# Windowed attention in unsplit fp32 on half arrays, its weights turned on VectorE and through DRAM

## The chip, the cores and the metric

One core of a Trainium2 chip runs the whole program: TensorE (PE, with its weight loads shown apart as PEld), VectorE (DVE), ScalarE (ACT), GpSimd (POOL) and SyncE (SP, which issues most transfers). The metric is device time in microseconds (us). The kernel before took 868.0 us, the median of three runs between 867.7 and 868.03.

## The reference

Attention over 4 sequences of 576 tokens, 8 heads of 64, with a causal window of 128 tokens and a linear bias, and then a dense mixture of 4 experts over the 2304 tokens of width 512:

```python
scores = scale * np.matmul(q, k.transpose(0, 1, 3, 2))
mask = (rel >= 0) & (rel < window)                      # window = 128
scores = np.where(mask, scores + bias[None], -1000000000.0)
attn = np.exp(scores - np.max(scores, axis=-1, keepdims=True))
attn = attn / (np.sum(attn, axis=-1, keepdims=True) + 1e-09)
x = np.matmul(attn, v)            # then heads side by side: (2304, 512)
for e in range(E):                # 4 experts, F = 1024
    h = np.maximum(x @ w1[e], 0.0)
    out += p[:, e:e + 1] * (h @ w2[e])
```

## The kernel before

**Split products.** TensorE multiplies one-pass "fp32r" operands here. To keep fp32 accuracy an operand is split into a rounded high part (a cast, `cast`, L380 on ACT or L381 on DVE) and the remainder (`minus`, L400 on DVE or POOL), and a product is the sum of several one-pass products of parts.

**Tiles.** The 2304 tokens stand in 18 tiles of 128 queries, and these in seven blocks (`BLOCKS`: three of 256 tokens, four of 384). Four head pairs times seven blocks make 28 segments (`segment`), each of two or three units (`unit`): one tile of queries for two heads. A unit's keys are its own tile and the 128 before it (fewer at a sequence's start). The first block is "plain": its four segments already use unsplit fp32 operands with 64 rows a head (L679) and 64 output columns a head (L921 with `acc,v`). The other 24 segments, with 64 units, are the ones in question.

**A unit before the change.** Scores: four one-pass matmuls (L688), per head the high and the low keys against queries whose high and low parts are stacked on 128 rows. `copy_predicated` (L742) folds the keys of the tile before and the own tile into 128 columns, since every query sees exactly 128 of the 256. DVE adds the bias and takes the least (L751), ACT takes the exponential (L769), and the weights are scaled by the reciprocal of their sum (L799 on DVE or L806 on ACT). TensorE transposes the two 128x128 blocks (L824) into a PSUM bank; a cast and a `minus` take the high and low parts out, and two POOL selects (L862) unfold them into `pt`, one for the tile before and one for the own tile. Values (L921): per head one-pass products of both parts of `pt` with `vs`, the high and low values side by side in 128 columns; the two halves of the output are added afterwards (ACT L948, DVE L951). Blocks 4 to 6 share accumulators in chains (`CHAINS`).

**The experts.** The first products (L1300, L1392) and second products (L1803) run in the same program order, and later passes use seven products in place of eight (L1449, L1699); DVE and POOL make the sums and remainders for them. These matmuls fill TensorE between the attention's.

**What sets the order.** Every operation is recorded in a `Plan` with its duration, its due time and what it reads and writes. `order()` then simulates the engines and emits each engine's instructions in the order that it finds; on the chip every engine runs its list in that order and waits by semaphores. SP issues its transfers in the listed order too. `FILL` = 80 small bf16 matmuls on `ones` (L1870) are put where the plan leaves TensorE free.

Of the kernel before, what the change touches and what calls it, by code (L numbers as in the profile page):

```python
# [27 lines left out]
class Buf:  # L28


    def __init__(self, tag):
        self.tag, self.place, self.uses, self.done, self.free = tag, None, 0, 0, 0.0
# [5 lines left out]
class Op:  # L38
    __slots__ = ("n", "engs", "emit", "due", "deps", "outs", "wait", "ready", "bufs", "cold", "start", "end", "eng", "port", "late", "lag", "after", "made")


class Plan:
# [12 lines left out]
    def op(self, engs, emit, due, reads=(), writes=(), holds=(), cold=None, port=None, late=0.0, lag=0.0, after=()):  # L55
# [5 lines left out]

        o.port, o.late, o.lag = (POOL,) if port is None else port, late, lag
# [27 lines left out]
    def order(self):  # L90
        at = dict.fromkeys((PE, DVE, ACT, POOL, SP), 0.8)
        queue = {e: [] for e in at}
        bus = port = 0.0
        landed = [0.0] * FLIGHT
# [7 lines left out]
        def slots(o):  # L102

            t, taken = -1.0, []
            for b in o.bufs:
                if b.place is not None:
                    continue
# [18 lines left out]
        while len(out) < len(self.ops):  # L126
            best = None
            for e, q in queue.items():
                cands, least = [], None
                for o in q:  # L130
# [3 lines left out]
                    t = max(at[e], o.ready[e], s[0] + 0.2 if s[1] else 0.0)  # L134
# [6 lines left out]
                if least is None:  # L141
                    continue
                t, o, taken = min(
                    (c for c in cands if c[0] <= least + SLACK), key=lambda c: (c[1].due, c[1].n)
# [33 lines left out]
            new = [b for b in o.bufs if b.place is None]  # L178
            for b, (tag, i) in zip(new, taken):
                owner[tag][i] = b  # L180
                b.place = self.places[tag][i]
# [14 lines left out]
AGAIN = 8.82  # L196
# [3 lines left out]
PLAIN = 4.0  # L200
FLIGHT = 9
SLACK = 0.1
PATIENCE = 0.4
HOLDOFF = 12.0
OPENS = 4.0
FAR = 3.0
EXTRA = 0.03
LATE_S = 2.02
LATE_T = .5
LATE_V = 1.34  # L210
# [27 lines left out]

CHAIN = (4, 5, 6)
CHAINS = ((2, (4,)), (3, (4,)), (0, (4, 5, 6)), (1, (4, 5, 6)), (2, (5, 6)), (3, (5, 6)))  # L240
ALONE = (0, 1, 2), (0, 2, 4), (1, 3, 5)
HEAD = (1, 2, 3), (0, 2, 4), (1, 3, 5)
PLACES = {
    1: (ALONE,),
    2: (HEAD, ALONE),
    3: (HEAD, ((0, 1, 2), (0, 2, 4), (1, 3, 1)), ((3, 0, 1), (4, 2, 1), (3, 0, 5))),
}
# [24 lines left out]
def attention_moe(  # L272
# [30 lines left out]
    def places(tag, n, shape, dt, pool_=sb):  # L303
# [10 lines left out]
    places("s", 3, [P, 2, 2 * P], F32)  # L314
    places("t", 6, [P, 6], F32)
    pt = sb.tile([P, 2, 2, 2 * QN], F32R, tag="pt", name="pt")
    plan.places["th"], plan.places["tl"] = (
        [plan.places[t][i][:, :, :QN] for t in ("qs", "kh", "kl")] + [pt[:, 0, i, :].rearrange("p (k n) -> p k n", k=2)]
        for i in range(2)
    )  # L320
    plan.places["s7"] = [pt[:, 1], vs[:].rearrange("p i t a d -> p i (t a d)")[:, :, :768]]
# [187 lines left out]
    turns = [(nb, hp) for hp, nbs in CHAINS for nb in nbs]  # L509
    for nb, (s0, n) in enumerate(BLOCKS):  # L510
        for hp in range(NPAIR):
# [4 lines left out]
            mine = next((c for h, c in CHAINS if h == hp and nb in c), (nb,))  # L516
            g.turn = turns.index((nb, hp)) if nb in CHAIN else -1
            g.open, g.behind, g.over = nb != mine[-1], nb != mine[0], None
            g.cols, g.prev, g.own = PLACES[len(mine)][mine.index(nb)]
            g.kn, g.vn = s0 + n - g.k0, (s0 + n) // P - g.v0 - g.open  # L520
            for i in range(n // P):
# [6 lines left out]
                if nb in CHAIN:  # L528
                    lo_, hi_ = spans[CHAIN[0]][0], spans[CHAIN[-1]][1]
                    at_ = turns.index((nb, hp)) * (n // P) + i  # L530
                    u.due = lo_ + (hi_ - lo_) * at_ / (len(CHAIN) * NPAIR * (n // P)) - MARGIN
                else:
                    u.due = lo_ + (hi_ - lo_) * (hp * (n // P) + i) / (NPAIR * (n // P)) - (MARGIN if nb else 0)
# [3 lines left out]

    for g in gs:
        if g.behind:
            g.over = next(x for x in gs if x.nb == g.nb - 1 and x.hp == g.hp)  # L540
# [16 lines left out]
    def segment(g):  # L557
# [4 lines left out]
        if g.plain:  # L562
            if g.hp % 2 == 0:
                shared = Buf("k"), Buf("v"), Buf("av")
# [6 lines left out]
            g.av = Part(shared[2], lambda t: t.place[half], half)  # L571
        else:
            k, v = g.k, g.v = Buf("k"), Buf("v")
        g.qs, g.kh, g.kl, g.vs = Buf("qs"), Buf("kh"), Buf("kl"), Buf("vs")
# [15 lines left out]
        else:  # L590
            q, g.qo = Buf("q"), 0
            g.q = q
            load(
                lambda: k[r, :, :kn],
                lambda: kd[hs, r, g.k0 : g.k0 + kn].rearrange("h p c -> p h c"),
                8 * r.stop * kn,
                due - 6,
                ["qk"],
                [k],
            )  # L600
            load(
                lambda: q[r, :, :n],
                lambda: qd[hs, r, g.s0 : g.s0 + n].rearrange("h p c -> p h c"),
                8 * r.stop * n,
                due - 6,
                ["qk"],
# [1471 lines left out]
```

## Time and profile before

| what | value |
|---|---|
| median of three runs | 868.0 us |
| profiled execution, span | 866.3 us |
| PE busy | 860.7 us (99%) |
| DVE, ACT, POOL busy | 706.9, 491.1, 494.6 us |
| PE's share of the chain that ended last | 97% |

The span is the profiled execution's own time from its first to its last instruction; the page has no other time for that execution, and the 1.7 us between span and median are what lies around it and between executions. A row of instructions on TensorE gives the start, and a length that holds the time through the array as well; since matmuls follow each other before the one ahead has come out, the time that one costs is the distance to the next start, not its length.

### The profile page before, as it was taken

The page shows a single profiled execution, that of the slowest core. Times are in us where ns is not written, and L with a number is a line of the kernel's source. Part 1 is how long each engine was busy: PE and PEld are TensorE (multiplying, and loading weights), DVE is VectorE, ACT ScalarE, POOL GpSimd, SP SyncE. Part 2 cuts the span into 40 slices and gives each one's busy share as a digit, 9 for nine tenths or more (in the row PEclk, how much of TensorE's full clock was granted, in tenths as well). Part 3 has the DMA queues.
Part 4 walks back from the last instruction along what each step waited for, and adds up shares of the span by engine and source line. Part 5 has one row for each costly group of instructions (what it writes and reads, how often), then busy time and mean ns, then how long its engine had stood idle before and what let it go on. Part 6 is the DMA issues. An engine that isn't in the chain of part 4 may idle for free.

```text
span 866.3 us, 15295 instructions
## 1 busy us (share of the span) xinstructions
PE 860.7 (99%) x5154; PEld 785.7 (91%) x5154; DVE 706.9 (82%) x1610; ACT 491.1 (57%) x1231; POOL 494.6 (57%) x696
## 2 busy tenths in 40 slices
PE   9999999999999999999999999999999999999998
PEld 6999888888888889999989899899899999999998
DVE  7888777778787887878998887876878888788877
ACT  7877666567777686753444434443346554545542
POOL 4665776465667767564552222522755776586663
PEclk9999999999999999999999999999999999999999
DMA  8676654444444555222597566545374446345602
GB/s 271 197 256 195 215 181 142 126 133 134 146 141 149 174 154 173 68 77 88 194 368 270 192 259 219 211 156 206 131 256 149 132 157 219 126 131 183 196 25 73
DMA packets 52526, 148.87 MB, mean 172 GB/s; under 512 B 4960, under 2 KB 22112, under 8 KB 48736
## 3 DMA queue, kind: packets, MB, share of 16 engines
q1 hardware_dynamic: 46592, 118.35, 40.5%
q0 software_dynamic: 5632, 29.36, 10.4%
q8 instruction: 40, 0.66, 0.3%
q14 instruction: 38, 0.31, 0.1%
q10 hardware_dynamic: 224, 0.20, 0.1%
HBM read 112.23 MB, written 35.65 MB: 171 GB/s over the span
## 4 chain that ended last, share of the span: by engine, by line
PE 97%; DVE 1%; DMA 0%; SPq 0%; issue 0%; ACT 0%; DVEq 0%
PE b L1803 31%; PE b L1449 23%; PE b L1392 18%; PE b L1699 11%; PE av L921 4%; PE b L688 3%; PE b L824 2%; PE av L1699 2%; PE av L1449 1%; PE b L1870 1%; PE b L1300 1%; DVE xl L400 0%; DVE acc L1725 0%; PE b L679 0%; DMA k<-in_qk 0%; SPq L373 0%
## 5 line engine op out<-in xcount | busy, mean ns | idle before, releaser
L1803 PE MATMUL b<-w2h,halves 128*128 128x512 f32 x612 | 214.1, 397 | 0.0
L1392 PE MATMUL b<-xh,w 128*128 128x512 f32 (+2 forms) x576 | 160.4, 344 | 0.0
L1803 PEld LDWEIGHTS b<-w2h,halves 128*128 128x128 f32 x612 | 115.1, 188 | 20.8
L1821 DVE SCALAR_TENSOR_TENSOR acc<-b,prob,acc 128x512 f32<-128x512 f32 x136 | 101.3, 746 | 32.6 <-PE b L1803 32.0
L1803 PE MATMUL b<-w2l,halves 128*128 128x512 f32 x306 | 120.0, 392 | 0.0
L1392 PEld LDWEIGHTS b<-xh,w 128*128 128x128 f32 x576 | 102.7, 189 | 10.1
L1392 PE MATMUL b<-xl,w 128*128 128x512 f32 (+2 forms) x288 | 97.7, 339 | 0.0
L400 POOL TENSOR_TENSOR w<-w1r,w 128x256 fp32r<-128x256 f32 x86 | 64.4, 773 | 55.0 <-ACT w L380 16.6
L862 POOL TENSOR_SCALAR_AFFINE_SELECT pt<-s 128x512 fp32r<-128x512 f32 x120 | 77.0, 666 | 31.6 <-DVE s L400 12.8
L400 POOL TENSOR_TENSOR w2l<-w2r,w2h 128x256 fp32r<-128x256 f32 x80 | 59.0, 759 | 59.3 <-ACT w2h L380 32.2
L1462 ACT ACTIVATE s<-b 128x384 f32<-128x384 f32 x87 | 42.6, 490 | 71.5 <-PE b L1449 68.9
L1725 DVE SCALAR_TENSOR_TENSOR acc<-b,prob,acc 128x256 f32<-128x256 f32 x135 | 58.5, 475 | 11.5 <-PE b L1699 9.9
L769 ACT ACTIVATE s<-s,t 128x128 f32<-128x128 f32 x128 | 50.4, 395 | 29.7 <-DVE t L751 28.4
L1803 PEld LDWEIGHTS b<-w2l,halves 128*128 128x128 f32 x306 | 57.7, 188 | 7.7
L1349 ACT ACTIVATE halves<-b 128x256 fp32r<-128x256 f32 (+2 forms) x76 | 36.8, 485 | 47.0 <-PE b L1392 46.4
L1449 PE MATMUL b<-xh,w 128*128 128x384 f32 x200 | 59.3, 337 | 0.0
L1392 PEld LDWEIGHTS b<-xl,w 128*128 128x128 f32 x288 | 54.5, 189 | 4.7
L380 ACT ACTIVATE w2h<-w2r 128x512 fp32r<-128x512 f32 x93 | 55.9, 621 | 3.2 <-PE b L1803 2.5
L1356 DVE SCALAR_TENSOR_TENSOR halves<-b,halves 128x256 fp32r<-128x256 f32 (+2 forms) x76 | 41.9, 553 | 15.8 <-ACT halves L1349 15.1
L380 ACT ACTIVATE w<-w1r 128x512 fp32r<-128x512 f32 x75 | 44.3, 623 | 6.7 <-DVE w1r L1234 4.4
L921 PEld LDWEIGHTS av<-pt,vs 128*128 128x128 f32 x312 | 43.7, 189 | 3.3
L400 DVE TENSOR_TENSOR w2l<-w2r,w2h 128x512 fp32r<-128x512 f32 x62 | 46.2, 758 | 0.3 <-ACT w2h L380 0.2
(249 smaller groups left out, 2460.0 us busy)
## 6 DMA issues: line engine op xcount, KB each, us to landing
w2r<-in_w SPq DMA_DIRECT2D x59, 512.0 KB, 3.5
w1r<-in_w SPq DMA_DIRECT2D x43, 512.0 KB, 4.3
w<-parked POOLq DMA_DIRECT2D x16, 1024.0 KB, 5.3
parked<-w SPq DMA_DIRECT2D x13, 1024.0 KB, 4.7
q<-in_q SPq DMA_DIRECT2D x16, 384.0 KB, 3.6
k<-in_k SPq DMA_DIRECT2D x12, 512.0 KB, 4.5
vs<-parked POOLq DMA_DIRECT2D x8, 768.0 KB, 4.8
pt<-parked POOLq DMA_DIRECT2D x8, 768.0 KB, 4.7
```

Of the source, the lines that this page charges most:

```text
L380: return nc.scalar.activation(o(), i(), AF.Copy)
L400: by[e].tensor_tensor(out=x, in0=y, in1=f(z), op=ALU.subtract) for x, y, z in pieces(e, n, o(), a(), b())
L769: return lambda e: nc.scalar.activation(sv()[:, h, -m:], sv()[:, h, -m:], AF.Exp, bias=t[:, h : h + 1], scale=-1.0, accum_out=t[:, 2 + h : ...
L862: return lambda e: nc.gpsimd.affine_select(out=pt[:, :, :, c0 : c0 + P], in_=hl(), pattern=[[0, 4], [1, P] if own else [-1, P]], base=0, c ...
L921: nc.tensor.matmul(o_, v2, p_, start=not g.started[h], stop=True, skip_group_check=True)
L1392: nc.tensor.matmul(bk[:, :n], a[0][:, kt, fs], b[:, kt, cols], start=kt == 0 and i == 0, stop=kt == KT - 1 and i == 2,)
L1449: nc.tensor.matmul(bank[:, :n], x(k), y(k), start=new and k == 0 and i == 0, stop=k == 1 and i == 2, skip_group_check=True,)
L1462: {ACT: act(n)}, lambda e: nc.scalar.activation(pv(p), bank[:, :n], AF.Copy), at[0] - URGENT, [bank], [p]
L1699: nc.tensor.matmul(bank[bk][part]()[:, cs], a()[:, ns], b()[:, fi, :], start=new and i != 1 and fi == 0 and j == 0, stop=fi == 1 and j == ...
L1725: nc.vector.scalar_tensor_tensor(out=ac[:, ds], in0=bank[bk][part]()[:, cs], scalar=prob[:, nt, e_ : e_ + 1], in1=ac[:, ds], op0=ALU.mult, ...
L1803: nc.tensor.matmul(bk[:, cs], a[:, ns], b[1][:, fi, cs], start=half != 1 and fi == 0 and j == 0, stop=half != 0 and fi == 1 and j == 2, sk ...
L1821: nc.vector.scalar_tensor_tensor(out=o, in0=i_, scalar=p, in1=o, op0=ALU.mult, op1=ALU.add)
```

## The change

Per unit of the 24 segments that are not plain:

- Queries and keys are no longer split. Their loads bring each head's 64 rows once (head 0 on rows 0 to 63, head 1 on rows 64 to 127), and scores are two unsplit fp32 matmuls on 64 rows each, one a head (L649 of the new program), each into its own bank. One planned operation does two neighbouring units.
- The transposes on TensorE are gone. DVE turns the weights in 32x32 blocks (`nc.vector.transpose`), the result goes to a DRAM scratch `tr`, and four transfers read it back with the blocks in their turned places. POOL's two selects then unfold it into `pb` without a split.
- Values are unsplit fp32 matmuls with 64 output columns a head (L903), all of a segment in one planned operation at its last unit, into one PSUM bank; nothing has to be added afterwards. Chains are gone.
- All eight PSUM banks are in the pool `b`.
- The planner knows three modes of TensorE ("full", "row", "col"), counts `SWITCH` for a change of mode, and while in a half-array mode prefers other half-array work (`STICK`). A dozen of its constants have other values. The expert products are the same instructions in the same numbers.

```diff
-    places("b", 6, [P, 512], F32, ps)
-    av = [[ps.tile([P, 512], F32, tag=f"av{h}", name=f"av{h}") for h in range(2)]]
-    plan.places["av"] = av
+    places("b", 8, [P, 512], F32, ps)
+    places("tr", TURNS, [P, 2 * P], F32, dr)
...
+                t, o, taken = min(
                     (c for c in cands if c[0] <= least + SLACK),
+                    key=lambda c: (c[1].due + (0.0 if c[1].mode == "full" else -STICK if sticks else lone), c[1].n),
                 )
...
+                if e == PE and t >= WARM:
+                    o.end += SWITCH if o.mode != mode else 0.0
+                    mode = o.mode
...
+            both = lambda t, c, m: t[hs].rearrange("h p c -> (h p) c")[64:192, c : c + m]
+            load(lambda: k[:, 0, :kn], lambda: both(kd, g.k0, kn), 512 * kn, due - 6, ["qk"], [k])
+            load(lambda: q[:, 0, :n], lambda: both(qd, g.s0, n), 512 * n, due - 6, ["qk"], [q])
...
-        cast(lambda: g.kh[:, :, :kn], lambda: k[:, :, :kn], 2 * kn, due, [k], [g.kh])
-        cast(lambda: g.qs[:, :, :n], lambda: q[:, :, :n], 2 * n, due, [q], [g.qs])
-        minus(
...
-                for m in (g.kh, g.kl):
+            for x in mine:
+                c0 = 0 if g.plain else 2 * P * (x.q0 // P % 2)
+                for h in range(2):
                     r = (lo64, hi64)[h]
+                    qv, kv = (g.q, g.k) if g.plain else (g.q[:, 0], g.k[:, 0])
                     nc.tensor.matmul(
+                        scored[h][:, c0 : c0 + x.pk + P],
+                        qv[r, g.qo + x.q0 : g.qo + x.q0 + P],
+                        kv[r, x.k0 : x.k0 + x.pk + P],
...
+                plan.op(
+                    {DVE: dve(2 * P) + 0.02},
+                    lambda e: nc.vector.transpose(
+                        turned_().rearrange("p (b h c) -> p h b c", b=4, h=2), sv().rearrange("p h (b c) -> p h b c", b=4)
+                    ),
...
+                load(lambda: tr[:], turned_, 131072, d + 0.8, [(wb, b_) for b_ in range(4)], [tr])
+                for b_ in range(4):
+                    load(
+                        lambda b_=b_: wb.place[32 * b_ : 32 * b_ + 32, :].rearrange("r (a n) -> r a n", a=4),
+                        lambda b_=b_: tr[:, 64 * b_ : 64 * b_ + 64].rearrange("(a r) n -> r a n", a=4),
+                        32768,
...
+            if pk:
+                for own in (0, 1):
+                    plan.op({POOL: 0.47}, side(own), d + 0.95 + 0.2 * own, raws_, [(g.pt, 2 * i + own)])
...
+                    d_ = (lo64, hi64)[h]
+                    p_ = g.pt[h][:, c : c + m] if g.plain else turned(c // P, (c + m) // P, h)
+                    nc.tensor.matmul(
+                        g.av[d_, q0 : q0 + m],
+                        g.v[:, vt, d_],
+                        p_,
...
-LATE_V = 1.34
+LATE_V = 1.699
```

TensorE's list before, among the experts' second products (L1803, with `halves` the hidden layer). L688 is one unit's scores, L921 values and L824 another unit's two transposes:

```order
L688 MATMUL b_116<-kh_71,qs_69 128x256
L688 MATMUL b_116<-kl_73,qs_69 128x256
L688 MATMUL b_116<-kh_71,qs_69 128x256
L688 MATMUL b_116<-kl_73,qs_69 128x256
L1803 MATMUL b_117<-w2h_99,halves 128x512
L1803 MATMUL b_117<-w2l_101,halves 128x512
L1803 MATMUL b_117<-w2h_99,halves 128x512 x2
L1803 MATMUL b_117<-w2l_101,halves 128x512
L1803 MATMUL b_117<-w2h_99,halves 128x512
L921 MATMUL av_119<-pt,vs 128x128 x2
L921 MATMUL av_120<-pt,vs 128x128 x2
L824 MATMUL b_115<-ident,s_76 128x128 x2
```

Scores, values and transposes came a unit at a time, with expert matmuls between. After, at a place among first products (L1338, the former L1392):

```order
L1338 MATMUL b_117<-xh_89,w_97 128x512
L903 MATMUL b_116<-pb_85,v_67 64x128 x2
L903 MATMUL b_116<-pb_85,v_67 64x256 x4
L903 MATMUL b_116<-pb_85,v_67 64x128 x2
L649 MATMUL b_121<-k_66,q_64 128x256
L649 MATMUL b_119<-k_66,q_64 128x256
L649 MATMUL b_118<-k_65,q_63 128x128
L649 MATMUL b_120<-k_65,q_63 128x128
L649 MATMUL b_118<-k_65,q_63 128x256
L649 MATMUL b_120<-k_65,q_63 128x256
L1338 MATMUL b_115<-xh_89,w_98 128x512
```

A whole segment's values (L903, eight matmuls) now stand right ahead of the scores of three units (L649, six matmuls), then experts follow; no transposes are left here. Over the whole list the 24 segments' values are 24 runs of column-half matmuls and their scores 25 runs of row-half matmuls, and these 49 runs stand in 27 blocks between full-array matmuls that are not there for a plain segment's values already. Of the 80 fillers on `ones`, 34 stand ahead of the last plain values (60 before), 29 in later places (20 before), and 17 behind the last expert matmul (none before).

SP's list before, early among the attention, with weight loads (`in_w`) and a segment's queries, keys and values:

```order
L373 DMA w1r_92<-in_w 128x1024
L373 DMA v_68<-in_v 128x384
L373 DMA q_63<-in_q 128x2x256
L373 DMA w2r_94<-in_w 128x1024
L373 DMA k_65<-in_k 128x2x384
L373 DMA w1r_93<-in_w 128x1024
L373 DMA w2r_95<-in_w 128x1024
L373 DMA v_67<-in_v 128x384
```

The same stage after; `tr` is the DRAM scratch, `s` the turned weights:

```order
L393 DMA tr_122<-s_77 128x256
L393 DMA w2r_96<-in_w 128x1024
L393 DMA k_65<-in_k 128x384
L393 DMA q_63<-in_q 128x256
L393 DMA tr_123<-s_78 128x256
L393 DMA w1r_93<-in_w 128x1024
L393 DMA s_77<-tr_122 32x4x64 x4
L393 DMA w2r_95<-in_w 128x1024
L393 DMA tr_124<-s_78 128x256
L393 DMA s_78<-tr_123 32x4x64 x2
```

Between the same loads stand a unit's store to the scratch and its four loads back, 320 issues in all, and the loads of queries and keys have half the size. In the stretch shown, a weight load is queued behind every load back, which itself waits for its store to land.

## Rows read from the trace of the kernel before

**Rows 1.** The page: span, busy time by engine, the chain that ended last.

```profile
span 866.3 us, 15295 instructions
...
PE 860.7 (99%) x5154; PEld 785.7 (91%) x5154; DVE 706.9 (82%) x1610; ACT 491.1 (57%) x1231; POOL 494.6 (57%) x696
...
PE 97%; DVE 1%; DMA 0%; SPq 0%; issue 0%; ACT 0%; DVEq 0%
```

**Rows 2.** Windows: stretch, us, busy us (instructions) by engine, clock, DMA share, GB/s.

```profile
0.00:26.00 26.00, 24.39 (x178) 17.90 (x179) 19.46 (x86) 20.07 (x64) 12.41 (x26) 1.00 0.83 267
26.00:391.00 365.00, 365.00 (x2125) 320.85 (x2125) 297.51 (x825) 253.81 (x733) 235.08 (x348) 1.00 0.49 155
```

**Rows 3.** PE groups by form: instructions, count | busy us, mean ns | idle.

```profile
L921 PE MATMUL av<-pt,vs 128*128 128x256 f32 x184 | 29.4, 282 | 0.0
L688 PE MATMUL b<-kh,qs 128*128 128x256 f32 x104 | 28.7, 297 | 0.0
...
L824 PE MATMUL b<-ident,s 128*128 128x128 f32 x128 | 24.6, 273 | 0.0
...
L921 PE MATMUL av<-pt,vs 128*128 128x128 f32 x128 | 17.9, 262 | 0.0
```

**Rows 4.** Timeline, PE: a unit's scores between experts. Start, us, what.

```profile
209.34 0.28 PE L688 MATMUL b<-kh,qs 128*128 128x256 f32 x1
...
209.82 0.39 PE L1803 MATMUL b<-w2h,halves 128*128 128x512 f32 x1
210.05 0.39 PE L1803 MATMUL b<-w2l,halves 128*128 128x512 f32 x1
```

**Rows 5.** Timeline, PE: a unit's two transposes.

```profile
202.44 0.38 PE L824 MATMUL b<-ident,s 128*128 128x128 f32 x2
202.58 0.48 PE L1392 MATMUL b<-xh,w 128*128 128x512 f32 x1
202.89 0.40 PE L1392 MATMUL b<-xl,w 128*128 128x512 f32 x1
```

**Rows 6.** Timeline, PE: four narrow values.

```profile
200.62 0.56 PE L921 MATMUL av<-pt,vs 128*128 128x128 f32 x4
201.02 0.45 PE L1392 MATMUL b<-xh,w 128*128 128x512 f32 x1
201.31 0.39 PE L1392 MATMUL b<-xl,w 128*128 128x512 f32 x1
```

**Rows 7.** Timeline, PE: plain scores of one pair, 128 columns.

```profile
12.68 0.49 PE L679 MATMUL b<-k 64*128 64x128 f32 x4
13.10 0.44 PE L824 MATMUL b<-ident,acc 128*128 128x128 f32 x2
```

**Rows 8.** Timeline, PE: fillers, plain values, plain scores, experts.

```profile
14.14 0.49 PE L1870 MATMUL b<-ones 128*128 128x256 bf16 x3
14.56 0.99 PE L921 MATMUL av<-acc,v 128*64 128x256 f32 x8
15.49 0.70 PE L679 MATMUL b<-k 64*128 64x256 f32 x4
16.12 0.39 PE L1300 MATMUL b<-xh,w 128*128 128x256 f32 x1
16.34 0.28 PE L1300 MATMUL b<-xl,w 128*128 128x256 f32 x1
```

**Rows 9.** Groups by form, DVE: remainders of the transposed weights.

```profile
L400 DVE TENSOR_TENSOR s<-b,s 128x256 fp32r<-128x256 f32 x60 | 25.2, 420 | 1.4 <-ACT s L380 0.5
```

**Rows 10.** DMA issues: count, size, median us to landing.

```profile
aside<-x SPq DMA_DIRECT2D x8, 192.0 KB, 1.9
...
ident<-in_ident SPq DMA_DIRECT2D x1, 64.0 KB, 2.7
dp<-in_dp SPq DMA_DIRECT2D x1, 36.0 KB, 4.0
```

**Rows 11.** Timeline, SP: an issue that waits for nothing.

```profile
6.17 0.43 SPq L373 DMA_DIRECT2D w1r<-in_w  x1
```

More of the change, by code (lines that the diff above doesn't have):

```diff
@@ L38 @@
 class Op:
-    __slots__ = ("n", "engs", "emit", "due", "deps", "outs", "wait", "ready", "bufs", "cold", "start", "end", "eng", "port", "late", "lag", "after", "made")
+    __slots__ = ("n", "engs", "emit", "due", "deps", "outs", "wait", "ready", "bufs", "cold", "start", "end", "eng", "port", "late", "lag", "after", "made", "mode")
 class Plan:
@@ L93, in order @@
         bus = port = 0.0
+        mode = "full"
         landed = [0.0] * FLIGHT
@@ L105, in slots @@
             for b in o.bufs:
-                if b.place is not None:
+                if b.slot is not None:
+                    t = max(t, b.since)
                     continue
@@ L177, in order @@
                 o.end += o.lag
-            new = [b for b in o.bufs if b.place is None]
+            new = [b for b in o.bufs if b.slot is None]
             for b, (tag, i) in zip(new, taken):
+                b.since = owner[tag][i].free if owner[tag][i] else -1.0
                 owner[tag][i] = b
-                b.place = self.places[tag][i]
+                b.slot = self.places[tag][i]
             for b in o.bufs:
@@ L195 @@
 CLOSE = 1.0
-AGAIN = 8.82
+AGAIN = 1.498
 DBW = 2.4e5
@@ L515, in attention_moe @@
             g.v0 = g.k0 // P
[L516 to L520, printed above, removed]
+            g.kn, g.vn = s0 + n - g.k0, (s0 + n) // P - g.v0
             for i in range(n // P):
@@ L697, in unit @@
-        passes_ = PLAIN if g.plain else 4
-        plan.op({PE: passes_ * mm(n)}, scores, d, qk, [*scored, "scores"], [s], passes_ * mmc(n), late=late)
+        qk = [(g.shared[0], g.hp % 2, h) for h in range(2)] if g.plain else [g.q, g.k]
+        if mine:
+            plan.op(
+                {PE: sum(PLAIN * mm(x.pk + P) for x in mine)},
+                scores,
+                d,
+                qk,
+                [*scored, "scores"],
+                [] if not g.plain else [s],
+                sum(PLAIN * mmc(x.pk + P) for x in mine),
+                late=late,
+                mode="row",
+            )
@@ L870, in side @@
                 )
-            plan.op({POOL: 0.79}, side(0), d + 1.1, both, [("pt", g.prev[i])])
-            plan.op({POOL: 0.59}, side(1), d + 1.2, both, [("pt", g.own[i])])
+            if pk:
+                for own in (0, 1):
+                    plan.op({POOL: 0.47}, side(own), d + 0.95 + 0.2 * own, raws_, [(g.pt, 2 * i + own)])
+            else:
+                cast(
+                    lambda: spread(2 * i + 1),
+                    lambda: wb.place,
+                    2 * P,
+                    d + 1.0,
+                    raws_,
+                    [(g.pt, 2 * i + 1)],
+                )
@@ L924, in unit @@
+                    d_ = (lo64, hi64)[h]
[4 more added lines that the diff above has]
+                        p_,
+                        start=not g.started[h],
+                        stop=True,
+                        skip_group_check=True,
+                    )
+                    g.started[h] = True
         if jobs:
+            if g.plain:
+                ps_ = [(b_, k_) for j in jobs for k_ in j[4] for b_ in g.pt]
+            else:
+                ps_ = [(g.pt, x) for x in range(2 * len(g.units)) if x or g.units[0].pk]
```

422 lines of the change are left out of this document (160 added, 262 removed).

## The prediction

> **What bounds the kernel now.** I read the page first. It gives a span of 866.3 us in which TensorE is busy for 860.7, and TensorE holds 97% of the chain that ended last [rows 1]. The windows say the same by stage: in the stretch with attention, 26 to 391 us, TensorE is busy for all of its 365.0 us at the full granted clock (1.00, the 2.4 GHz level), while DVE is at 297.5, ACT at 253.8 and POOL at 235.1 [rows 2]. So nothing but TensorE's own work, and what would make it wait, counts there; work that leaves DVE, ACT and POOL is worth nothing by itself. Only the first 26 us have another limit, since there TensorE partly runs fillers. Then I counted the attention's matmuls by form [rows 3] and took their prices from the timeline, as distances between starts [rows 4 to 8].
>
> **TensorE's work that goes.** Four score matmuls of 256 columns start at 209.34 and the next expert matmul at 209.82, which then takes its usual 0.23 (to 210.05): 0.48 a unit [rows 4]. Of the 64 units 52 have this form (104 matmuls with `kh`, two a unit [rows 3]): 25.0 us. The other 12 have 192 or 128 keys; I price them at 0.43, between four narrow matmuls (0.40) and 0.48: 5.2 us. Two transposes take from 202.44 to 202.58, and the expert matmul behind them needs 0.31 to the next start where 0.23 is usual: 0.14 + 0.08 = 0.22 a unit [rows 4, 5], and 128 of them [rows 3] are 64 pairs: 14.1 us. Values of 256 columns are 184, 46 fours at the 0.48 of the same shape: 22.1 us. Those of 128 are 32 fours: 0.40 from 200.62 to 201.02 and 0.06 on the expert matmul behind (0.29 in place of 0.23), 0.46 each [rows 6]: 14.7 us. Sum: 25.0 + 5.2 + 14.1 + 22.1 + 14.7 = 81.1 us.
>
> **TensorE's work that comes.** The plain block already runs both new forms. A pair of score matmuls on half rows takes 0.42 with 128 columns (12.68 to 13.10 [rows 7]) and 0.63 with 256 (15.49 to 16.12 [rows 8]). So 128 more columns for both heads together cost 0.21, which at 2.4 GHz is four passes of 128 (0.213): the heads run side by side. What is left, 0.21, is the price of a row run whatever its length. Per head there are 15,360 score columns (52 units of 256, 8 of 192, 4 of 128) and 15,872 value columns (40 matmuls of 256, 44 of 128), 244 times 128 in all: 244 x 0.213 = 52.0 us. This is as much column time as before: split products took four passes on the full array, unsplit ones take four on a half.
>
> What is gained is then the transposes and the fixed parts, and against them stand changes of mode. A column run of 256 and 128 columns a head lasts from 14.56 to 15.49, 0.93, of which 3 x 0.213 = 0.64 are columns: 0.29 a run [rows 8]. Into a block: three fillers 0.11 apart from 14.14 on would put the next start at 14.47, and it is 14.56: 0.09. Out of it: the first full matmul needs 0.22 (16.12 to 16.34) where 0.12 is usual for 256 columns (a quarter of rows 4's 0.48): 0.10 [rows 4, 8]. By the new order there are 25 row runs, 24 column runs and 27 blocks: 25 x 0.21 + 24 x 0.29 + 27 x 0.19 = 5.3 + 7.0 + 5.1 = 17.4 us. The new attention is 52.0 + 17.4 = 69.4 us, against 81.1: **11.7 us less**. Reading starts to 0.01 us leaves about 1.2 us either way (244 pieces at half of that).
>
> The Trainium skill (TensorE: Matmul & The Clock Gate, "The mechanism" in Part 3) says that matmuls on different tiles of the array start about 4 ns after each other, for row and column tiles alike. By that rule a column run would cost no more than a row run. The trace does not agree: 0.29 against 0.21 [rows 7, 8].
>
> **Other terms.** *Fillers.* Ahead of the last plain values 26 fillers less are placed, at 0.11 each 2.9 us. Whether that time really goes depends on the softmax chain in the first 26 us, where DVE was busy for 19.5 and ACT for 20.1 [rows 2], part of it with splits for the next block that are no longer made. Between 0 and 2.9 I take 2.0 less. Later 9 fillers more stand in places where the plan sees TensorE free: 1.0 more. The 17 behind the last matmul (1.9 us) lie beside the last sums and the last store, which lands no sooner than about 1.9 us after its issue [rows 10]: 0.
>
> *DVE.* The 32x32 turning does not occur in the trace. It takes the place of a remainder of the same 128x256 size, 60 of them at 0.42 [rows 9], and I take 0.42. From half of that to three times it, 64 of them are 13 to 81 us. At the upper end DVE would stand at 297.5 - 25.2 + 81 = 353 of 365 us [rows 2, 9], still under the window, and more than the remainders goes (splits of queries, keys and values, additions of halves). So: 0.
>
> *New waits.* Weights for a unit now pass through a store and four loads back before POOL can unfold them, and a segment's values wait for the last of its units. Behind them on TensorE stand its scores and the next experts; behind the selects on POOL stand remainders for the experts' weights. A store of 192 KB lands after 1.9 us and a load of 64 KB after 2.7 [rows 10], so a turn takes some 5 us; the planner puts the values late enough for its own estimate of that and adds `LATE_V` = 1.699. Bounds: nothing, or about 10 us (0.4 for each of 24 value operations). Before, nearly all such waits were planned away (TensorE is 365.0 of 365 busy), so I take 2.0, near the low end.
>
> **Sum.** -11.7 - 2.0 + 1.0 + 2.0 = -10.7 against the profiled execution's 866.3, or 855.6; the median of the runs stands 1.7 above this span, so 857.3 us.
>
> **Rivals.**
>
> *The turn comes late (slower).* Place: the wait of each segment's values on the last load back. The scratch is read in runs of 64 floats, 256 bytes. The nearest row, `dp` with 288-byte lines, landed after 4.0 us though it has 36 KB, against 2.7 for the 64 KB of `ident` [rows 10]. If each turn is 1.3 us later than planned beyond its margin, 24 x 1.3 = 31 us: 857.3 - 2.0 + 31 = 886 us. It decides from 0.5 us a segment on (24 x 0.5 = 12, the gain). Against it: `dp` was queued in the opening at a DMA share of 0.83, where the attention has 0.49 [rows 2], and the plan has its margin. The Trainium skill (DMA: Bandwidth & Descriptors, "Specifications") asks for at least 512 bytes a transfer for full rate, which speaks for this rival; that `dp` was slow agrees with it, but the row can't tell short lines from the full queues.
>
> *SP's queue takes the gain (no change).* SP gets 320 issues more at 0.43 [rows 11]: 138 us. A load back holds the queue until its store has landed, at most 64 x 1.9 = 122 us [rows 10], and some 150 of its former issues are 65: 325 of 365 us. It fits, but with 0.6 us more a unit it is full, and from there each further 0.17 a unit delays weight loads and holds TensorE for 11 us (64 x 0.17): about 867. Against it: weight loads are issued well ahead, and other loads stand between store and load back.
>
> *The column runs get cheaper, and all fillers of the opening go.* 24 x (0.29 - 0.21) = 1.9 and 0.9, with no new waits another 2.0: 852.5. For it: the price rests on one run of a few pieces in the opening, and the new runs are longer; against it: that row.
>
> *The halves don't run side by side.* Then 52 us come on top: 909. Rows 7 and 8 exclude it for the plain block.
>
> **How the numbers follow.** Forecast 0.72, slower rival 0.08, SP rival 0.12, cheaper runs 0.07, no pairing 0.01. A measurement of this kernel tells 0.2%, 1.7 us, from no change. Faster by more has the forecast and the cheaper runs, 0.79; within 0.2% the SP rival, 0.12; slower 0.09. Range: at the low end 857.3 - 1.2 - 0.9 - 2.0 = 853.2; at the high end no opening gain and 10 us of waits, 857.3 + 2.0 + 8.0 = 867.3. So 853 to 867; outside are the slower cases and the cheapest runs.
>
> **What would show it.** TensorE busy for nearly the whole span, with equal prices for expert matmuls; no transposes past the opening; column runs near 0.29 and row runs near 0.21 above their columns; scores no later than the matmuls ahead allow. The plain segments' values should end earlier than before. Wrong would be: idle time of TensorE ahead of L903 ended by POOL's selects or a load from `tr`; weight loads that land when the experts already wait; or runs at twice their columns.

## The result, and the profile after

The changed kernel takes 860.3 us (median of 4 runs, 859.7 to 860.7) against 868.0 (867.7 to 868.3) for the kernel before on the same chip: ratio 0.9909, 95% interval 0.9895 to 0.9923. The prediction was 857.3 us, 853 to 867. The profiled execution's span is 857.9 us, 8.4 less than before.

The page of the changed kernel, to be laid beside [rows 1]: span, busy time by engine, the chain that ended last.

```profile
span 857.9 us, 15239 instructions
...
PE 849.4 (99%) x5050; PEld 750.1 (87%) x5050; DVE 674.5 (79%) x1622; ACT 384.3 (45%) x1001; POOL 365.9 (43%) x573
...
PE 92%; DVE 5%; ACT 1%; DMA 1%; SPq 1%; issue 0%
```

ACT and POOL lost over 100 us of work each, which the sum of the gain at the end does without. But TensorE's share of the chain fell from 97% to 92% and DVE's rose from 1% to 5%: somewhere TensorE now waits for DVE. The windows tell where (stretch, us, busy us and instructions by engine, clock, DMA share, GB/s):

```profile
26.00:391.00 365.00, 364.97 (x2092) 298.28 (x2092) 272.72 (x854) 157.28 (x519) 121.31 (x237) 1.00 0.61 180
620.00:858.00 238.00, 231.69 (x1644) 227.91 (x1642) 196.22 (x374) 114.30 (x240) 144.77 (x206) 1.00 0.42 139
```

The stretch with attention is as full as before [rows 2]; the idle time is in the last stage, where the change altered none of TensorE's instructions, only the order of the engines' lists. The waits of TensorE in the whole span (what waited, for what; us in total, times, longest) name the place:

```profile
PE b L1654 <- ACT s L1408: 3.9, 6, 0.7
PE b L1825 <- DVE ones L1809: 1.1, 1, 1.1
PE b L903 <- ACT acc L400: 0.6, 1, 0.6
PE b L649 <- DVE t L724: 0.4, 1, 0.4
```

The second row is at the program's start, the third and fourth in the opening. The first is six waits, one in each pair of experts of the last stage. The view counts only time with no matmul in the array; by starts, each of the six is 0.82 us longer than a step, and a smaller gap of 0.22 stands about 5 us ahead of each: 6.2 us in all.

The new operations, in the groups by form, and in the list of DMA issues (count, size, median us to landing):

```profile
L824 DVE STREAM_TRANSPOSE s<-s 128x256 f32<-128x256 f32 x64 | 28.1, 440 | 10.9 <-POOL pb L856 10.3 <-ACT t L737 0.3
```

```profile
tr<-s SPq DMA_DIRECT2D x64, 128.0 KB, 2.8
s<-tr SPq DMA_DIRECT2D x256, 32.0 KB, 2.8
```

A turn costs DVE 0.44 us, where 0.42 was taken from [rows 9]. Store and loads land after 2.8 us each, later than the 1.9 and 2.7 of [rows 10]; still no row of the waits above names L903 behind a select or a load.

Last, the two kinds of run on TensorE (start, length, what). A column run with 768 columns a head, and a row run with 512:

```profile
354.09 1.52 PE L903 MATMUL b<-pb,v 128*64 128x128 f32 x16
355.54 0.39 PE L1338 MATMUL b<-xh,w 128*128 128x256 f32 x1
...
302.67 1.13 PE L649 MATMUL b<-k,q 64*128 64x256 f32 x8
303.74 0.50 PE L1758 MATMUL b<-w2h,halves 128*128 128x512 f32 x1
```

355.54 - 354.09 = 1.45, of which six times 0.213 = 1.28 are columns: 0.17 a column run. 303.74 - 302.67 = 1.07, less four times 0.213 = 0.85: 0.22 a row run. The other runs past the opening agree: all 24 column runs cost 0.165 to 0.171, and all row runs but one 0.21 to 0.23.

### The profile page after: what moved, and what is told of

Its sections match the earlier page's. It is cut to its first block, busy times and chain, and to the rows that moved or that the text cites. A ratio compares the mean times of both kernels' runs of the same rounds, so it can differ in the third digit from the quotient of the medians.

```text
span 857.9 us, 15239 instructions
## 1 busy us (share of the span) xinstructions
PE 849.4 (99%) x5050; PEld 750.1 (87%) x5050; DVE 674.5 (79%) x1622; ACT 384.3 (45%) x1001; POOL 365.9 (43%) x573
## 3 DMA queue, kind: packets, MB, share of 16 engines
q0 software_dynamic: 5632, 29.36, 10.7%
## 4 chain that ended last, share of the span: by engine, by line
PE 92%; DVE 5%; ACT 1%; DMA 1%; SPq 1%; issue 0%
PE b L1758 31%; PE b L1395 23%; PE b L1338 18%; PE b L1654 11%; PE b L903 4%; PE b L649 4%; DVE xl L420 2%; DVE acc L1680 1%; DVE b L1424 1%; DVE w1r L1568 1%; PE b L1246 1%; DMA w1r<-in_w 1%; PE b L1825 1%; SPq L393 1%; ACT xh L1563 0%; ACT s L1408 0%
## 5 line engine op out<-in xcount | busy, mean ns | idle before, releaser
L1758 PE MATMUL b<-w2h,halves 128*128 128x512 f32 x612 | 207.5, 394 | 0.0
L1338 PE MATMUL b<-xh,w 128*128 128x512 f32 (+2 forms) x576 | 153.8, 341 | 0.0
L1338 PEld LDWEIGHTS b<-xh,w 128*128 128x128 f32 x576 | 102.2, 189 | 14.7 <-issue 1.5
L856 POOL TENSOR_SCALAR_AFFINE_SELECT pb<-s 128x256 f32<-128x256 f32 x120 | 52.7, 465 | 123.5 <-DMA s<-tr 47.5
L1338 PE MATMUL b<-xl,w 128*128 128x512 f32 (+2 forms) x288 | 97.6, 339 | 0.0
L1680 DVE SCALAR_TENSOR_TENSOR acc<-b,prob,acc 128x256 f32<-128x256 f32 x156 | 66.6, 473 | 9.4 <-PE b L1654 8.2
L1395 PE MATMUL b<-xh,w 128*128 128x384 f32 x232 | 68.8, 337 | 0.0
L400 ACT ACTIVATE w2h<-w2r 128x512 fp32r<-128x512 f32 x81 | 49.2, 624 | 30.2 <-PE b L1758 28.3
L420 POOL TENSOR_TENSOR w2l<-w2r,w2h 128x256 fp32r<-128x256 f32 x54 | 40.8, 776 | 50.8 <-ACT w2h L400 24.1
L1338 PEld LDWEIGHTS b<-xl,w 128*128 128x128 f32 x288 | 54.4, 189 | 6.1
L420 DVE TENSOR_TENSOR w2l<-w2r,w2h 128x512 fp32r<-128x512 f32 x75 | 52.3, 723 | 1.2 <-ACT w2h L400 0.8
L1654 PE MATMUL b<-w2h,xh 128*128 128x256 f32 x144 | 41.3, 287 | 3.9 <-ACT s L1408 3.9
L1395 PEld LDWEIGHTS b<-xh,w 128*128 128x128 f32 x232 | 42.8, 188 | 0.6
```

What stands on the lines that cost most here:

```text
L400: return nc.scalar.activation(o(), i(), AF.Copy)
L420: by[e].tensor_tensor(out=x, in0=y, in1=f(z), op=ALU.subtract) for x, y, z in pieces(e, n, o(), a(), b())
L856: return lambda e: nc.gpsimd.affine_select(out=spread(2 * i + own), in_=wb.place, pattern=steps, base=0, channel_multiplier=-sign, compare ...
L1338: nc.tensor.matmul(bk[:, :n], a[0][:, kt, fs], b[:, kt, cols], start=kt == 0 and i == 0, stop=kt == KT - 1 and i == 2,)
L1395: nc.tensor.matmul(bank[:, :n], x(k), y(k), start=new and k == 0 and i == 0, stop=k == 1 and i == 2, skip_group_check=True,)
L1654: nc.tensor.matmul(bank[bk][part]()[:, cs], a()[:, ns], b()[:, fi, :], start=new and i != 1 and fi == 0 and j == 0, stop=fi == 1 and j == ...
```

## The experiments

All ratios are against the kernel before on the same chip, which took 868.1 to 868.2 us there. "Pair" is a pair of experts of the last stage, of which there are six.

**What the six waits are.** Around one of them in the changed kernel: the timelines of DVE and POOL 8 us ahead of it, then of TensorE, with ACT and DVE beside it (in square brackets the idle time ahead):

```profile
745.19 2.25 DVE L420 TENSOR_TENSOR xl<-w1r,xh 128x384 fp32r<-128x384 f32 x1
...
744.98 0.57 POOL L1085 DMA_DIRECT2D w<-parked  x1
745.57 1.44 POOL L420 TENSOR_TENSOR xl<-w2r,xh 128x256 fp32r<-128x256 f32 x2
...
747.49 0.39 PE L1654 MATMUL b<-w2h,xl 128*128 128x256 f32 x1
...
752.18 0.34 PE L1395 MATMUL b<-xh,w 128*128 128x384 f32 x1
753.17 0.35 PE L1654 MATMUL b<-w2h,xh 128*128 128x256 f32 x1 [0.66 <-ACT s L1408]
...
752.55 0.49 ACT L1408 ACTIVATE s<-b 128x384 f32<-128x384 f32 x1 [1.84 <-PE b L1395]
...
752.16 1.25 DVE L1680 SCALAR_TENSOR_TENSOR acc<-b,prob,acc 128x256 f32<-128x256 f32 x3
```

The ACT operation that the profile names reads another bank than the one that the waiting matmul writes. That bank is read by the first two of DVE's three weighted sums (L1680), which end at about 753. (In a_port, below, the same matmul follows the same L1395 without a gap, at 718.62, while that ACT operation begins only at 718.82: it does not wait for ACT.) DVE is late, and the row that stands out is a remainder of 2.25 us; remainders of this size take 0.63 on average in the kernel before (below). The smaller gap ends right behind it: the remainder is over at 747.44, and a matmul that reads `xl` starts at 747.49. Three explanations were tried: the order on DVE (a constant of the planner), the new bank pool, and POOL's two operations that run beside the long remainder.

**Runs a_ahead2 and b_ahead2.** The same constant, set back in the changed kernel and set forward in the kernel before:

```diff
-AHEAD2 = 4.943      # a_ahead2; in b_ahead2 1.95 becomes 4.943
+AHEAD2 = 1.95
```

> The changed kernel with one planner constant set back: AHEAD2 1.95 in place of 4.943 (how much earlier than the weighted sums the remainders of the last experts' sums are due on DVE). The order of every engine is the changed kernel's up to the last experts' stage. In the changed kernel TensorE stands there six times for 0.82 us and six times for 0.22 us between L1395 and L1654, 6.2 us in all. Theory A (DVE order: remainders L420 are put ahead of the weighted sums L1680 that free the PSUM bank): the twelve waits go, 860.3 - 6.2 = 854.1 us (853.5 to 855.5). Theory B (the bank pool: the two banks that were set apart for values are now drawn from one pool, so a bank is written again sooner, whatever DVE does first): the waits stay, 859.5 to 861 us.

> The kernel before with that one constant of the changed kernel: AHEAD2 4.943 in place of 1.95, nothing else. Theory A (DVE order): waits of about 0.8 us between L1449 and L1699 appear in the last experts' stage, in each of its six pairs, 868.0 + 5 to 7 = 873 to 875 us. Theory B (bank pool): the banks are as before, so no waits: 867.5 to 868.5 us.

Measured: a_ahead2 868.9 us (ratio 1.0007, 0.9998 to 1.0016), b_ahead2 877.2 us (1.0104, 1.0090 to 1.0118). b_ahead2 got the very waits, 0.78 us in each pair, and a long remainder ahead of each, with the banks of before: the pool is not needed for them. It took 2 us more than the range expected; two more waits, of 0.75 and 1.25 us, stand outside the pairs (646.66 and 857.22). DVE, then POOL, in b_ahead2:

```profile
763.19 2.35 DVE L400 TENSOR_TENSOR xl<-w1r,xh 128x384 fp32r<-128x384 f32 x1
...
763.03 0.57 POOL L1139 DMA_DIRECT2D w<-parked  x1 [0.18 <-issue]
763.61 1.44 POOL L400 TENSOR_TENSOR xl<-w2r,xh 128x256 fp32r<-128x256 f32 x2
```

a_ahead2 missed its number by 14.8 us: the waits did not go, one of 1.3 us in each pair and another of 0.7 to 1.4 from the third pair on took their place, and its remainders are long too (0.86 us on average). So no single value of this constant makes or mends the waits; it moves DVE's work against POOL's, and with the changed kernel's other constants 1.95 moves it to a worse place.

**Run a_const.** All of the planner's constants that both kernels have, as before:

```diff
-MARGIN = 8.948
+MARGIN = 15.32
...
-URGENT = 8.93
+URGENT = 6.0
...
-AHEAD2 = 4.943
+AHEAD2 = 1.95
```

> The changed kernel's structure with every planner constant that both kernels have set to the value before. By the order it has 42 row runs, 28 column runs and 44 mode blocks in place of 28, 28 and 33. At the prices of the prediction (0.21 a row run, 0.19 into and out of a block) that is 14 x 0.21 + 11 x 0.19 = 5.0 us more in the attention. Theory A (constants set the waits in the last experts' stage): these 6.2 us go, 860.3 + 5.0 - 6.2 = 859.1 us (857 to 861). Theory B (bank pool): they stay, 865.3 us (863.5 to 867).

Measured: 859.1 us (ratio 0.9899, 0.9885 to 0.9912). In the last stage one wait of 0.2 us is left between L1395 and L1654, while 44 mode blocks in place of 33 made the attention dearer. This is the changed structure alone, and it is as fast as the changed kernel (1.2 us apart, where its own runs spread over 2.5), so the retuned constants won nothing together: fewer changes of mode, paid back in the last stage. That the expected number was met so closely is partly luck, since waits of 0.5 and 1.1 us that the sum doesn't have stand ahead of L1395 (414.56 and 526.09).

**Run a_port.** One line that tells the planner that these remainders, which it let run beside anything, use what POOL's operations use:

```diff
-    def minus(o, a, b, n, due, reads, writes, gp=True, after=()):
+    def minus(o, a, b, n, due, reads, writes, gp=True, after=(), own=()):
...
-        return plan.op(engs, emit, due, reads, writes, port=(DVE, POOL) if gp else (), after=after)
+        return plan.op(engs, emit, due, reads, writes, port=(DVE, POOL) if gp else own, after=after)
...
-            first_[i, fi] = minus(lo, r_, h, n, ready[i], [rk, hk], [lk], i > 2, [first_[2, fi]] if i == 3 else ())
+            first_[i, fi] = minus(lo, r_, h, n, ready[i], [rk, hk], [lk], i > 2, [first_[2, fi]] if i == 3 else (), (DVE,))
```

> The changed kernel, with one thing told to its planner: that a DVE remainder of the last experts' sums (L420 called from L1587, 128x384, two SBUF operands) uses what POOL's tensor operations use too, so that POOL's are not placed beside it. TensorE's and SP's order are word for word the changed kernel's. In the changed kernel and in the kernel before with AHEAD2 4.943, one such remainder in each of the six pairs lasts 2.25 (2.35) us in place of 0.57, over the whole course of two POOL operations of 0.75 us that began 0.38 us after it, and TensorE stands 0.82 + 0.22 us a pair. Theory C (the DVE operation is held while POOL runs beside it, and the sums behind it free the bank late): no remainder over 0.7 us there, the twelve waits go, 860.3 - 6.2 = 854.1 us (853.5 to 856). Theory D (the length of that remainder is only an effect of something else DVE waits for, such as the ACT cast before it): waits stay, 859.5 to 861 us.

Measured: 852.5 us (ratio 0.9818, 0.9805 to 0.9832), the fastest level reached here and 7.8 us under the changed kernel, with TensorE's list unchanged. That is below the range expected, so the waits cost more than the 6.2 us counted: matmul by matmul, a_port is 0.1 us ahead of the changed kernel at 647 us and 7.4 at 855, 7.3 gained in the last stage. Its page, and then the timelines of DVE and POOL at the same place of a pair:

```profile
span 851.1 us, 15245 instructions
...
PE 99%; SPq 0%; DMA 0%; DVE 0%; issue 0%
```

```profile
711.77 0.55 DVE L420 TENSOR_TENSOR xl<-w1r,xh 128x384 fp32r<-128x384 f32 x1
...
711.57 0.57 POOL L1085 DMA_DIRECT2D w<-parked  x1
712.47 1.44 POOL L420 TENSOR_TENSOR xl<-w2r,xh 128x256 fp32r<-128x256 f32 x2 [0.32 <-DVE xl L420]
```

POOL now waits 0.32 us for the remainder, which takes 0.55, and DVE's share of the chain is 0%. The remainder ran beside POOL's DMA issue here without loss, so what held it was the two tensor operations.

**Run b_port.** The same line in b_ahead2:

> The kernel before with AHEAD2 4.943 (877.2 us, with one DVE remainder of 2.35 us and 0.78 + 0.28 us of waits a pair) and, as in a_port, the planner told that DVE's remainders in the last experts' sums use what POOL's operations use. Theory C (the DVE operation held beside POOL makes the waits): remainders back at 0.55 to 0.7 us, the waits go, 877.2 - 9.0 = 868.2 us (867 to 869.5), no faster than the kernel before, which has no such waits. If the order that AHEAD2 makes costs by itself: 873 to 877 us.

Measured: 867.9 us (ratio 0.9999, 0.9990 to 1.0008): 9.3 us back, and no gain over the kernel before, which has no such waits to lose. The remainders as one group (count | busy us, mean ns) in before, changed, a_port, b_ahead2 and b_port:

```profile
L400 DVE TENSOR_TENSOR xl<-w1r,xh 128x384 fp32r<-128x384 f32 x32 | 20.0, 634 | 0.0
```

```profile
L420 DVE TENSOR_TENSOR xl<-w1r,xh 128x384 fp32r<-128x384 f32 x32 | 28.4, 908 | 0.3 <-ACT xh L400 0.3
```

```profile
L420 DVE TENSOR_TENSOR xl<-w1r,xh 128x384 fp32r<-128x384 f32 x32 | 16.9, 566 | 0.0
```

```profile
L400 DVE TENSOR_TENSOR xl<-w1r,xh 128x384 fp32r<-128x384 f32 x32 | 30.0, 958 | 0.0
```

```profile
L400 DVE TENSOR_TENSOR xl<-w1r,xh 128x384 fp32r<-128x384 f32 x32 | 17.4, 577 | 0.1
```

The mean of this one group tells the kernels with the waits (0.91, 0.96) from those without (0.57 to 0.63).

**Run a_late6.** Six constants that act on the last stages, as before:

```diff
-PATIENCE = 0.645
+PATIENCE = 0.4
-HOLDOFF = -2.753
+HOLDOFF = 12.0
-OPENS = 2.874
+OPENS = 4.0
-FAR = 1.744
+FAR = 3.0
-WLATE = 9.01
+WLATE = 8.47
-AHEAD2 = 4.943
+AHEAD2 = 1.95
```

> The changed kernel with six planner constants of before that act on the last experts' stages (AHEAD2 1.95, WLATE 8.47, PATIENCE 0.4, FAR 3, OPENS 4, HOLDOFF 12). TensorE's order is the changed kernel's up to the fillers at 624 us, so the attention stays as it is. The kernel with all constants of before (859.1 us) had no wait between L1395 and L1654. Theory C (POOL beside DVE; these constants put the two apart): the 6.2 us of waits go, 854.1 us (853.5 to 856). If instead the waits need the other constants of before as well (URGENT 6): as the changed kernel or slower, 860 to 868 us, as with AHEAD2 alone (868.9).

Measured: 853.3 us (ratio 0.9833, 0.9820 to 0.9846), just under the range expected. Another order, in which the longest of these remainders takes 0.96 us (0.67 on average), gives nearly the same time, by moving work rather than by naming the conflict. One wait in the attention is of another kind: scores that wait 0.89 us for their queries' load.

```profile
319.97 1.14 PE L649 MATMUL b<-k,q 64*128 64x256 f32 x8 [0.89 <-DMA q<-in_q]
```

**Run a_direct.** Part of the turn undone: `DIRECT = 0x111111`.

> The changed kernel with the weights of 16 of its 64 units past the opening turned on TensorE (32 transposes) and copied out of PSUM by ACT, in place of a DVE turn and a way through DRAM (DIRECT=0x111111). By the prediction's price of 0.22 a unit (two transposes 0.14, the expert matmul behind them 0.08): 16 x 0.22 = 3.5 us more, 863.8 us (862.5 to 865.5). If the way through DRAM made values late on TensorE by as much as it takes transposes away, no change: 860 us. If an unsplit transpose also costs a change of mode, 16 x 0.19 = 3.0 more, 866.8 us.

Measured: 863.9 us (ratio 0.9948, 0.9936 to 0.9961), 3.6 over the changed kernel where 3.5 was expected. For these 16 units the way through DRAM gives back nothing of what the transposes cost.

**Run a_stick0.** Mode changes no longer avoided:

```diff
-STICK = 49.533
+STICK = 0
-AHEAD2 = 4.943
+AHEAD2 = 1.95
```

> The changed kernel with STICK=0 (the plan no longer gathers TensorE's half-array runs into blocks) and AHEAD2 1.95. By the order it has 40 row runs, 28 column runs and 62 blocks in place of 28, 28 and 33. If a row run costs 0.21 and a block 0.19 beside its columns, as the prediction took: 12 x 0.21 + 29 x 0.19 = 8.0 us more than the kernel with AHEAD2 1.95 alone. If a change of mode cost nothing: no difference to that kernel. If the fixed part belongs to the scores themselves and not to the run (a wait for operands): the blocks alone, 5.5 us more.

Measured: 888.3 us (ratio 1.0234, 1.0219 to 1.0250), 19.4 over a_ahead2 where 8.0 was expected. Of that, new waits for DVE are about 10.7 (gaps over 0.15 us between experts: 24.0 against 13.3), among them one of 3.3 and one of 2.2 us ahead of L1395. Behind both the granted clock fell to the lower of its two levels for a while; in the second of these stretches, with the clock as the last but two figures:

```profile
428.60:432.20 3.60, 3.16 (x10) 3.16 (x11) 2.89 (x6) 2.05 (x4) 2.30 (x4) 0.53 0.97 271
```

Matmuls of 384 columns start 0.32 us apart there in place of 0.18, and in the two stretches 1.6 us of this is not in the 10.7. The 7.1 that are left lie between two of the expectations (8.0 and 5.5), so the total is a weak test of the prices of runs and blocks.

**Run a_turnwise.** The order within a column run:

```diff
-            for vt, c, q0, m, _ in jobs:
-                for h in range(2):
+            for vt, c, q0, m, h in [(*j[:4], h) for h in range(2) for j in jobs] if not g.plain else [(*j[:4], h) for j in jobs for h in range(2)]:
+                if True:
```

> The changed kernel, with the value matmuls of each of its 24 column runs in another order: all of one head, then all of the other, in place of by turns. The work and all other engines' orders are the same. If two heads' matmuls run side by side on the two halves of the array because they are issued by turns: each head's 15,872 columns then run alone, 15,872 x 4 / 2.4 GHz = 26.5 us more, 886.7 us (885 to 889). If TensorE looked further ahead in its queue, or if the pair's price had another reason: within 2 us of 860.3.

Measured: 871.6 us (ratio 1.0040, 1.0026 to 1.0054): 11.3 more, neither of the two numbers. The run of the same work as the one at 354.09:

```profile
386.09 2.22 PE L903 MATMUL b<-pb,v 128*64 128x128 f32 x16
388.24 0.39 PE L1338 MATMUL b<-xh,w 128*128 128x256 f32 x1
```

It lasts 2.15 us. By turns it was 1.45, and one head after the other without overlap it would be 2 x 1.28 + 0.17 = 2.73. So the halves do run side by side, and TensorE also begins the second head's matmuls while some of the first head's are still to come. Each of the eight matmuls stands in the trace as two rows, 16 in all; their starts come in the sizes 128, 128, 256, 256, 256 and then 128 again, only 7 ns after the fifth, ahead of the first head's sixth. It does not look far enough to make the order indifferent.

**Run p_hop.** a_port with the turned weights stored to a second DRAM tile and copied from there to `tr`, unknown to the planner:

```diff
-                load(lambda: tr[:], turned_, 131072, d + 0.8, [(wb, b_) for b_ in range(4)], [tr])
+                    nc.sync.dma_start(out=mid[:], in_=turned_())
+                    return nc.sync.dma_start(out=tr[:], in_=mid[:])
+                plan.op({SP: 131072}, lambda e: there(), d + 0.8, [(wb, b_) for b_ in range(4)], [tr])
```

> The kernel a_port (852.5 us) with a longer way for the turned weights, of which the planner knows nothing: each unit's store goes to a second DRAM tile and from there by another DMA to the first, so that its loads back start one landing later, and SP has one issue and one more wait a unit. In the changed kernel's trace the last POOL select ended between 0.18 and 10.8 us before its column run on TensorE, 2.2 us in the middle. If that distance is the slack of the turn, 2.5 us more of way (its store and loads landed after 2.8 us each) makes TensorE wait where less than 2.5 is left: summed over the 24 runs 13.2 us, so 865.7 us (860 to 873). If the waits end up with SP (its queue is held a landing longer for each of 64 units, 64 x 2.5 = 160 us, and weight loads come late): above 880 us. If the turn had far more slack than these distances show: within 2 us of 852.5.

Measured: 967.5 us (ratio 1.1142, 1.1119 to 1.1165), 115 over a_port. The largest wait of SP and the two largest of TensorE (us in total, times, longest; L650 are the scores, L909 the values), and then SP's timeline at one unit:

```profile
SPq L836 <- DMA hop<-s: 156.7, 64, 5.8
...
PE b L650 <- DMA q<-in_q: 20.9, 5, 7.5
PE b L909 <- POOL pb L862: 14.9, 6, 4.3
```

```profile
63.55 0.38 SPq L835 DMA_DIRECT2D hop<-s  x1
67.41 0.47 SPq L836 DMA_DIRECT2D tr<-hop  x1
67.97 0.53 SPq L394 DMA_DIRECT2D w2r<-in_w  x1
```

SP stands until the hop has landed, and a load of weights stands behind it. 156.7 / 64 = 2.45 us a unit. The prediction's rival had SP's queue full from 0.6 us more a unit on: (2.45 - 0.6) x 64 = 118 us. The agreement in size speaks for that rival's mechanism, at a dose the change doesn't have, and so do the scores that wait for their queries' loads. It is not proof: with the added issue of 0.47 the same sum gives 148; TensorE also waits 14.9 us for selects ahead of the values, which is the place of the other rival, the turn that comes late; and TensorE's busy time rose, from 846.2 to 885.3 us for as many instructions, at a granted clock of 0.88 in the stretch from 100 to 200 us. The windows of that stretch in p_hop and in a_port:

```profile
100.00:200.00 100.00, 77.56 (x379) 59.02 (x375) 52.20 (x185) 31.41 (x113) 25.83 (x54) 0.88 0.55 159
```

```profile
100.00:200.00 100.00, 100.00 (x560) 79.78 (x561) 72.97 (x249) 42.03 (x148) 28.40 (x58) 1.00 0.59 172
```

**Runs p_latev0 and p_sent.** a_port with `LATE_V = 0`, and a_port with `SENT = 0.57`:

> The kernel a_port with LATE_V=0 in place of 1.699, the time that the plan puts between the last select that it foresees and a segment's values. By the order it has 25 column runs, 28 row runs and 33 blocks, as a_port but for the column runs (28 with the opening's). If the plan's own durations of the turn are right without the margin: no difference, 852.5 us within 1.5. If the margin covers what the plan foresees too short: with the distances of the changed kernel's trace, 1.7 us less of them leaves TensorE waiting 5.4 us in 8 of the 24 runs, 857.9 us (855 to 862).

> The kernel a_port with the planner's time for an issue of POOL's DMA set to what the trace shows, SENT 0.57 in place of 1.0. In the last experts' stages POOL has 4 such issues a pair; the plan then lets POOL's remainders start up to 0.43 us earlier. If something there still waits for POOL in the plan alone: 852.5 - 0.5 to 1.0, 851.5 to 852.0 us. If nothing on TensorE's path hangs on it: 852.5 within 1 us.

Measured: 853.1 us (ratio 0.9823, 0.9808 to 0.9837) and 852.4 us (0.9812, 0.9798 to 0.9827), neither distinguishable from a_port. The planner's estimate of the turn holds without the margin of 1.7 us. To take these 1.7 us off the distances between select and column run, as the expectation did, foretold 5.4 us of waits that did not come: the planner sets a new order, and a distance read in the old one doesn't tell what the new one leaves.

## Why the prediction was right, and where not

*TensorE's attention: right in kind, 2.9 us too small.* The row run was priced at 0.21 and takes 0.22. Each of the 27 blocks was priced at 0.09 in and 0.10 out, and in the trace they take 0.09 to 0.10 and 0.10 to 0.11. The column run was priced at 0.29 and takes 0.17: 24 x 0.12 = 2.9 us. The step that failed is the choice of row: the run at 14.56 [rows 8] was taken as typical. In that run the second head's first matmul starts 0.13 us after the first's (14.56 and 14.69), and the same plain work later in the trace of before is quicker:

```profile
23.36 0.87 PE L921 MATMUL av<-acc,v 128*64 128x256 f32 x8
24.16 0.39 PE L688 MATMUL b<-kh,qs 128*128 128x256 f32 x1
```

24.16 - 23.36 = 0.80, less 0.64 of columns: 0.16, with the two heads 7 ns apart. That row was there to be read. The plain weights of the two heads are cast separately, the new ones lie in one tile; that the late head waited for its cast is likely, not tested. In the new runs too the heads start 7 ns apart (6 in row runs), so the Trainium skill's rule (TensorE: Matmul & The Clock Gate, "The mechanism" and "Measured speedup vs the span model" in Part 3: some 4 ns between tiles, row or column alike) is borne out, and the sentence that the trace does not agree was wrong. With 0.17 the prediction's own formula gives 52.0 + 25 x 0.21 + 24 x 0.17 + 27 x 0.19 = 66.5, so -14.6 in place of -11.7. The rival of the cheaper column runs was right in this one of its three terms.

*Transposes.* 0.22 a unit is confirmed by a_direct (3.6 against 3.5).

*Halves side by side.* Confirmed by the 1.45 of the column runs; that rival is out.

*Opening, taken as -2.0.* The first second product starts at 29.92 against 29.21, but by then 6 units of the later scores are done in place of 2; at 1.07 for two units [as at 302.67] that is -1.4 for equal work. The executions of a_port and a_late6, with the same TensorE order up to there, pass the mark at 29.68 and 28.89, so a single execution cannot settle this term. The sign that the prediction gave for it failed: the last of the plain values' runs starts later, at 24.56 against 23.36, with the scores of four units of later segments ahead of it.

*Later fillers, +1.0.* As counted: 29 against 19 beyond the opening, without those behind the last matmul; what they cost was not measured apart.

*DVE, 0; turn and SP, waits of +2.0.* DVE's price was right and its share fell from 82% to 79%. No wait stands at the turn. One of 0.3 us stands among scores (in a row run at 318.55); no view names what ended it, but in a_late6 a wait at the same place ended with a load of queries, which SP issues. The two rivals about the turn and SP did not happen; p_hop shows what 2.45 us more a unit do, and no run shows where between 0 and that the loss sets in.

*The waits came elsewhere.* The prediction looked for new waits only where the change adds instructions, and took the expert stages as equal. The retuned constants reorder DVE and POOL there, and cost 6.2 us by the gaps. Sum by what was measured: -14.6 - 1.4 + 1.0 + 6.2 + 0.3 = -8.5, beside the 8.4 of the spans. So close an agreement is partly luck: laid beside a_port, the last stage lost 7.3, not 6.2, and the kernel before had waits of 0.3 and 0.4 us there itself (646.25 and 853.27). The forecast of 857.3 was near because two misses of opposite sign, 2.9 too little gain and waits of 6.5 us in place of 2.0, partly cancel; with the last stage mended the change is worth 15.6 us (a_port).

## What to carry to other kernels

When a change comes with retuned scheduling constants, treat every stage that they reorder as changed, and compare the means of identical instruction groups between the two traces: one group of remainders at 0.91 in place of 0.63 us pointed at the loss that the named releaser hid. A planner that leaves out one shared resource for one kind of operation works until its order happens to put the two side by side; telling it costs a line. And a price read from one run of several should be read from all of them, the cheapest first.

## What the runs showed of the hardware

A DVE subtraction of two SBUF operands (128x384) takes 0.55 us alone and 2.25 to 2.35 beside two POOL tensor operations of 0.75; POOL's take the same in both cases (means 0.745 and 0.736). The Trainium skill (SBUF — State Buffer, "Who interferes with whom") says that a DVE instruction with two SBUF inputs and a GpSimd one that reads SBUF exclude each other, and that the later one blocks. The exclusion agrees; but the held DVE operation is recorded as beginning 0.38 us ahead of POOL's (745.19 and 745.57), and it stayed held across the boundary between two POOL operations. That is not always so: in a_ahead2 a remainder recorded at 785.53, just behind the start of a POOL operation, came through between two of them, with 1.10 us.

TensorE starts matmuls of one half of the array ahead of earlier ones for the other half: in a_turnwise, 2.15 us for a run that would take 2.73 in strict order.

Idle stretches cost twice: in p_hop the granted clock was at the lower of its two levels (1.2 in place of 2.4 GHz) for part of each stretch of the attention (mean 0.88 to 0.95), and TensorE's work itself was 39 us longer. In a_stick0 the same can be seen one wait at a time: behind the idle 3.3 us that end at 429.04, matmuls started 0.32 us apart in place of 0.18.
